# One order of waits and one DMA queue model in the planner of a two-branch attention kernel

## The chip, the cores and the metric

The kernel runs on one core of one Trainium2 chip. The time is that of the device for one execution, in microseconds (us); for the kernel before it is 681.26 us, the median of five runs (679.8 to 682.55). A difference of 0.2% (1.36 us) is about what can be told from no change.

Engines, by their short names: PE is TensorE (PEld its weight loads), ACT is ScalarE, DVE is VectorE, POOL is GpSimd, and SP is SyncE, whose only work here is to issue DMAs.

## The reference, cut to what matters

```python
x = A_x                                              # [1, 2048, 512], bf16, 32 heads of 16
g = sigmoid((x * gate_w).sum(-1, keepdims=True))
# branch A: softmax attention
q, k, v = split(x @ A_wqkv)                          # each [32 heads, 2048, 16]
o = softmax(q @ k.T * 16 ** -0.5) @ v
a = merge(o) @ A_wo
# branch B: linear attention
q, k, v = split(x @ B_wqkv)
pq, pk = phi(q), phi(k)                              # phi(t) = where(t > 0, t + 1, exp(t)) + 1e-6
num = pq @ (pk.T @ v);  den = pq @ pk.sum(rows) + 1e-6
b = merge(num / den) @ B_wo
return g * a + (1 - g) * b
```

## The kernel before, in words

Branch A makes 32 x 2048 x 2048 exponentials, and they are most of the work. They are cut into units of 128 keys x 512 queries of one head. Four heads make a round (there are 32 rounds of 64 units each, so 2048 units); a unit's scores are one matmul that reads `KT` and `Qz`. The exponential of a unit is made in one of two ways. ACT takes two units at a time from PSUM banks 0 and 1 or 2 and 3, as one `ACTIVATE` of 128x1024 that writes a slot of `P` (`cand_exp`, line 771 of the profile; "exp" below). Or DVE takes one unit from bank 4 or 5 by an addition that makes the bits of a power of two (`cand_op1`, line 685), and two shifted copies of it are made, by POOL (line 739) or by DVE (line 749), in tiles `Z`. PE then multiplies `P` and `Z` with the values `Vc` (`cand_pv`) and adds up in bank 7. A group of two matmuls for ACT and, mostly, one for DVE is called a score wave here (`cand_s`).

Everything else (projections, branch B, the final products) is written as tasks: generators that yield one step after another, with a round at which each is released and one at which it is due. Their steps fill the gaps. They share PSUM bank 6 until the very end (`owner`).

**The planner.** The function does not write instructions as it goes. It runs a model of the engines: each engine has a time at which it is free, each tile (`_Res`) the time at which its last writer and its readers end (`tw`, `tr`), and `_avail` gives the earliest start of a step on an engine. In a loop it collects what could be done next on each engine, picks one by the modelled start and by priorities, and emits it. So the order of instructions on every engine is fixed when the program is built, and it depends on the modelled durations. On the chip each engine goes through its own list in that order, held only by semaphores.

**Waits.** `deps_of` lists an instruction's dependencies: the writers of what it reads, then the writers and the readers of what it overwrites. `_Eng.add` (line 62) goes through that list, leaves out what the engine has already waited for, and keeps one wait for each semaphore, the highest value, in the order in which the semaphores first came up. A dependency is either an `_Ev` (an instruction of an engine) or a `_Raw` (a DMA's semaphore). `emit_engine` (line 1464) calls `wait_ge` for each wait and then the instruction. In the built program the first of the waits is carried by the instruction itself; the others, if there are any, go into one separate EVENT_SEMAPHORE instruction ahead of it, which belongs to line 1468. There are 716 of these on ACT, 578 on PE, 248 on POOL, 147 on DVE and 18 on SP.

**DMAs.** The planner's `dma` gives SP 60 ns for an issue (`issue`) and lets the data land a fixed time after it (`lat`), however many other DMAs were issued just before. Those that the loop at line 1450 issues on SP:

- `t_q` (names Q...): the projection of queries is written to `QT` by DVE (line 957) and spread to `Qz` by eight DMAs of 16 KB, `lat` 2500 ns; there are 15 such sets.
- `t_bout` (names BO...): for each of 16 row blocks, DVE writes the normalised branch-B rows to one of two slots `OBn`, which lie in the tile `wA0` (line 1163; the profile calls the tile `wA`), and a transposing DMA moves them to `OBT`, which lies in `xnat` (line 348), `lat` 3200 ns. The DVE step of block n overwrites the slot that the DMA of block n-2 reads, and so waits for it.
- `t_load` and `t_wo`: weights (WA, WB, WO) and rows of x (XN), `lat` 3500 and 5000 ns.
- `t_final` (names F...): the output rows, `lat` 2200 ns. `t_final` multiplies `OBT` and `OAT` with the output weights (line 377 through `mmt`) in bank 6.

The key lines of the waits and of the DMA model are

```python
        for d in deps:                                   # _Eng.add
            if d is None:
                continue
            ...
            start = max(E.free, _avail(E, reads, writes))    # dma
            E.free = start + issue
            fin = start + lat
```

Of the kernel before, what the change touches and what calls it, by code (L numbers as in the profile page):

```python
# [20 lines left out]
class _Raw:  # L21
    __slots__ = ("sem", "val")

    def __init__(self, sem, val):
        self.sem = sem
        self.val = val


class _Ev:
    __slots__ = ("E", "idx")  # L30

    def __init__(self, E, idx):
        self.E = E
        self.idx = idx


class _Eng:
# [23 lines left out]

    def add(self, fn, deps=(), inc=True, dma_sem=None):
        waits = []
        for d in deps:
            if d is None:
                continue
            if isinstance(d, _Raw):
                sem, val = d.sem, d.val
            else:
                sem, val = d.E.sem, d.E.cover(d.idx)  # L70
            key = id(sem)
            if val <= 0 or self.waited.get(key, 0) >= val:
                continue
            self.waited[key] = val
            for k, (s2, v2) in enumerate(waits):
                if s2 is sem:
                    if val > v2:
                        waits[k] = (sem, val)
                    break
            else:  # L80
                waits.append((sem, val))
        self.n += 1
        idx = self.n
        if inc:
            self.semval += 1
            self.inc_idx.append(idx)
            self.inc_val.append(self.semval)
        self.ops.append((waits, fn, inc, dma_sem))
        return _Ev(self, idx)


class _Res:

    __slots__ = ("name", "w", "r", "tw", "tr", "we", "late")
# [14 lines left out]
def _avail(E, reads, writes):  # L109
    t = 0.0  # L110
    for res in reads:
        if res.w is not None:
            x = res.tw if res.we is E else res.tw + LAT + (res.late if E.name == "pe" else 0.0)
            if res.we is E and E.name == "pe":
                x = 0.0
            if x > t:
                t = x
    for res in writes:
        if res.w is not None and res.we is not E:
            if res.tw + LAT > t:  # L120
                t = res.tw + LAT
        for e2, tr in res.tr.items():
            if e2 is not E and tr + LAT > t:
                t = tr + LAT
    return t


def bass_gated_mix__mha_block__linear_attn_block__prompt_kernel(
# [61 lines left out]
    with ExitStack() as es:  # L190
# [63 lines left out]
        SP = _Eng("sp", None, 0.0)  # L254
# [40 lines left out]
        def deps_of(E, reads, writes):  # L295
            deps = []
            for res in reads:
                if res.w is not None:
                    deps.append(res.w)
            for res in writes:  # L300
                if res.w is not None:
                    deps.append(res.w)
                deps.extend(res.r.values())
            if E is PE:
                deps = [d for d in deps if not (isinstance(d, _Ev) and d.E is PE)]
            return deps

        def emit(E, dur, fns, reads=(), writes=(), name=""):
            if callable(fns):
                fns = [fns]  # L310
            start = max(E.free, _avail(E, reads, writes))
            E.free = start + dur
            fin = start + dur + E.pipe
            deps = deps_of(E, reads, writes)
            if E is PO and gate[0] is not None:
                deps.append(gate[0])
            last[E] = None
            first = None
            for k, fn in enumerate(fns):
                ev = E.add(fn, deps if k == 0 else (), inc=(k == len(fns) - 1))  # L320
                if first is None:
                    first = ev
            last[E] = ev
            for res in reads:
                res.r[E] = ev
                res.tr[E] = fin
            for res in writes:
                res.w = ev
                res.we = E
                res.tw = fin  # L330
                res.r = {}
                res.tr = {}
            LOG.append((start, E.name, dur, name))
            RLOG.append((E.name, dur, E.pipe, [(d.E.name, d.idx) if isinstance(d, _Ev) else ("dma", id(d.sem), d.val) for d in deps if d is not None],
                         ev.idx, name, cur_mode[0] if E is PE else None))
            return fin

        dma_eng = {}

        def dma(E, o, i, sem, total, lat, reads=(), writes=(), transpose=False, noncontig=False, name="dma", issue=60.0):  # L340
            start = max(E.free, _avail(E, reads, writes))
            E.free = start + issue
            fin = start + lat
            eng = {"sp": nc.sync, "act": nc.scalar, "pool": nc.gpsimd}[E.name]

            def go():
                if transpose:
                    return eng.dma_start_transpose(o, i)
                if noncontig:
                    with nc.allow_non_contiguous_dma(reason="strided load"):  # L350
                        return eng.dma_start(o, i)
                return eng.dma_start(o, i)
            dd = deps_of(E, reads, writes)
            E.add(go, dd, inc=False, dma_sem=sem)
            raw = _Raw(sem, total)
            for res in reads:
                res.r[(E, id(sem))] = raw
                res.tr[(E, id(sem))] = fin
            for res in writes:
                res.w = raw  # L360
                res.we = SP if E is SP else None
                res.tw = fin
                res.r = {}
                res.tr = {}
            LOG.append((start, E.name, issue, name))
            RLOG.append((E.name, issue, lat, [(d.E.name, d.idx) if isinstance(d, _Ev) else ("dma", id(d.sem), d.val) for d in dd if d is not None],
                         ("dma", id(sem)), name, None))
            return fin
# [29 lines left out]
        for E, tbs in ((SP, (0, 1)), (AC, (2, 3))):  # L398
            for tb in tbs:
                dma(E, xnat[:, tb, :], x2[128 * tb:128 * (tb + 1), :], semX0[tb], 16, 3300.0, writes=[r_xn[tb]], issue=450.0)  # L400
        for k3 in (0, 1):
            dma(AC, wA0[:, :, k3, :], wsrc[:, :, k3 * D:k3 * D + 128], semW0[k3], 16, 3300.0, writes=[r_wA0[k3]], issue=450.0)
        for t in range(1, NQC):
# [5 lines left out]
            for h in range(2):  # L409
# [8 lines left out]
             reads=[r_ident], writes=[r_ident])  # L418
# [5 lines left out]
             reads=[r_pidx], writes=[r_pidx])  # L424
        emit(DV, 150, lambda: nc.vector.tensor_scalar(qmask[:, 1:2], pidx[:, 1:2], QS / 16.0, None, op0=ALU.mult),
             reads=[r_pidx], writes=[r_qmask])
        emit(DV, 150, lambda: nc.vector.tensor_scalar(qmask[:, 0:1], pidx[:, 1:2], -QS / 16.0, QS, op0=ALU.mult, op1=ALU.add),
             reads=[r_pidx], writes=[r_qmask])
# [5 lines left out]
        for (tile_, w_, rr) in ((bmask, 16, r_bmask), (zmask, 1, r_zmask)):  # L434
# [4 lines left out]
                reads=[rr], writes=[rr])  # L439
            emit(PO, 300, lambda ap=ap, w_=w_: nc.gpsimd.affine_select(  # L440
                out=ap, in_=ap, compare_op=ALU.is_ge, fill=0.0, base=15, pattern=[[16, 8], [0, w_]], channel_multiplier=-1),
                reads=[rr], writes=[rr])
        emit(PE, 3000, [mm(bank(b % 3 if b < 7 else 7), warm[:, 0:128], warm[:]) for b in range(8)], reads=[r_warm],
             writes=[r_bank[0], r_bank[1], r_bank[2], r_bank[7]])
# [140 lines left out]
        class C:  # L585
            __slots__ = ("E", "prio", "dur", "fns", "reads", "writes", "after", "name", "mode", "wt", "lock", "task")

            def __init__(self, E, prio, dur, fns, reads, writes, after, name, mode=None, wt=1.0, lock=False, task=False):
                self.task = task
                self.wt = wt  # L590
                self.lock = lock or E is PO
                self.E, self.prio, self.dur, self.fns = E, prio, dur, fns
                self.reads, self.writes, self.after, self.name, self.mode = reads, writes, after, name, mode
# [801 lines left out]
        while True:  # L1395
# [11 lines left out]
            for f in (cand_s, cand_dsolo, cand_pv, cand_op1, cand_shift, cand_pshift, cand_exp):  # L1407
                c = f()
# [8 lines left out]
            for c in cands:  # L1417
                a = _avail(c.E, c.reads, c.writes)
                start0 = start = max(c.E.free, a)
                if c.E is PE and c.mode and c.mode != st["mode"]:  # L1420
                    start = max(start, PE.free + SWITCH)
                if c.lock:
                    start = max(start, port["pool" if c.E is DV else "dve"])
# [7 lines left out]
                key = (max(start0, c.E.free + KEYW), -c.prio - (STICK if c.E is PE and c.mode == st["mode"] else 0.0))  # L1431
                if c.E not in by or key < by[c.E][0]:
                    by[c.E] = (key, start, c)
            key, start, c = min(by.values(), key=lambda v: v[1] - (BIAS if v[2].E is DV and v[2].lock else 0.0))
            if c.E is PE:
                fill(start, c.mode)
                start = max(start, PE.free + (SWITCH if c.mode and c.mode != st["mode"] else 0.0))
# [12 lines left out]
                port[c.E.name] = start + c.dur + 20.0  # L1450
            if isinstance(c.fns, tuple) and c.fns[0] == "DMA":
                _, o, i, sem, tot, lat, rd, wr, tr, chk = c.fns[1]
                fin = dma(SP, o, i, sem, tot, lat, reads=rd, writes=c.writes, transpose=tr, name=c.name)
                if not chk:
                    for res in wr:
                        res.tw = max(res.tw, fin)
            else:
                cur_mode[0] = c.mode
                fin = emit(c.E, c.dur, c.fns, c.reads, c.writes, name=c.name)
# [65 lines left out]
```

The softmax here doesn't subtract the row's maximum and nothing guards it: scores larger than these inputs give would overflow.

## Time and profile before

| | before |
|---|---|
| median of five runs | 681.26 us (679.8 to 682.55) |
| the profiled execution | 679.8 us |
| its span, first to last instruction | 677.7 us |
| granted PE clock | 1.00 |
| DMA, mean | 24 GB/s, 16 MB in all |

The profile counts an engine as busy from the start of an instruction to its end; on ACT and DVE the end of one overlaps the start of the next, so the mean duration of an exp, 1118 ns, is more than the 904 ns that lie between the starts of two exps that follow each other without a wait. A wait that an instruction carries itself is not shown as an instruction; an EVENT_SEMAPHORE is, as "PEldq L1468" or "DVEq L1468". The times of the planner and of the trace differ by a slowly growing offset (11.0 us at the trace's 551 us).

### The profile page before, as it was taken

To read this page: it belongs to the slowest core of one execution; us is meant where nothing else is said; L and a number is where in the kernel's file an instruction comes from. 1 tells how busy PE (TensorE), PEld (TensorE's weight loads), DVE (VectorE), ACT (ScalarE), POOL (GpSimd) and SP (SyncE) were. 2 spreads that over 40 slices of the span, in tenths; PEclk is the share of its full clock that TensorE was granted. 3 is DMA by queue.
4 is the path that set the end of the run, shared out by engine and by line. 5 is a ranking of instruction groups with operands and counts; after the bars stand their busy time and mean duration, and the time that the engine had idled before them with its cause. 6 is when DMAs were issued, how large, how long until landed. Compare 5 with 4: busy or idle time off the path is not lost.

```text
span 677.7 us, 24102 instructions
## 1 busy us (share of the span) xinstructions
PE 667.5 (98%) x9886; PEld 203.2 (30%) x9886; DVE 607.9 (90%) x1062; ACT 658.2 (97%) x734; POOL 550.7 (81%) x611
## 2 busy tenths in 40 slices
PE   8999999999999999999999999999999999999998
PEld 4322233323223232222333322232332332222222
DVE  6999999998899998999899888899998988899996
ACT  5899999999999999999999999999999999999995
POOL 3767878889878888888898888898788997887882
PEclk9999999999999999999999999999999999999999
DMA  6420001200000000000002000001020021000000
GB/s 133 134 89 8 4 2 38 66 10 3 2 10 1 10 2 2 10 2 2 12 3 65 10 10 1 10 17 22 7 34 9 14 48 31 17 16 11 26 17 32
DMA packets 27963, 15.96 MB, mean 24 GB/s; under 512 B 19792, under 2 KB 26832, under 8 KB 27856
## 3 DMA queue, kind: packets, MB, share of 16 engines
q1 hardware_dynamic: 26512, 13.91, 7.9%
q8 instruction: 79, 1.29, 0.8%
q10 hardware_dynamic: 1344, 0.52, 0.4%
q14 instruction: 28, 0.23, 0.1%
HBM read 6.69 MB, written 2.10 MB: 13 GB/s over the span
## 4 chain that ended last, share of the span: by engine, by line
PE 77%; ACT 13%; issue 5%; DVE 4%; DMA 0%; POOL 0%; ACTq 0%; DVEq 0%; POOLq 0%
PE ps L371 59%; PE ps L377 18%; ACT P L771 11%; DVE Z L685 2%; ACT eb L1056 1%; DMA xnat<-wA 0%; DVE T L1021 0%; DVE gnat L1013 0%; DVE QT L957 0%; DVE wA L1163 0%; PE ps L899 0%; DVE Z L749 0%; DVE OAT L1048 0%; POOL Z L739 0%; DVE rec L1040 0%
## 5 line engine op out<-in xcount | busy, mean ns | idle before, releaser
L771 ACT ACTIVATE P<-ps 128x1024 bf16<-128x1024 f32 x695 | 645.7, 1118 | 5.9 <-PE ps L371 5.8
L739 POOL TENSOR_TENSOR Z<-Z,mcon 128x512 int32<-128x512 int32 x465 | 480.4, 1058 | 81.4 <-DVE Z L685 49.1
L685 DVE TENSOR_SCALAR Z<-ps 128x512 int16<-128x512 f32 x659 | 441.0, 684 | 53.3 <-PE ps L371 45.3
L371 PE MATMUL ps<-Z,Vc 128*17 128x512 bf16 x1977 | 282.4, 382 | 0.3
L371 PE MATMUL ps<-Qz,KT 32*128 32x512 bf16 x2048 | 272.2, 384 | 3.4 <-DVE Z L685 1.0
L371 PE MATMUL ps<-P,Vc 128*17 128x512 bf16 x1389 | 250.1, 383 | 0.2
L371 PEld LDWEIGHTS ps<-Qz,KT 32*128 32x128 bf16 x2048 | 68.5, 91 | 259.2 <-ACT P L771 235.0
L371 PEld LDWEIGHTS ps<-Z,Vc 128*17 128x17 bf16 x1977 | 63.8, 88 | 79.4 <-issue 52.6
L749 DVE TENSOR_SCALAR Z<-Z 128x1024 int16<-128x1024 int16 x195 | 81.2, 432 | 0.2
L371 PEld LDWEIGHTS ps<-P,Vc 128*17 128x17 bf16 x1389 | 56.3, 88 | 55.4 <-issue 40.7
L371 PE MATMUL ps<-warm 128*32 128x512 bf16 (+15 forms) x600 | 62.4, 326 | 1.2 <-DVE dummy L420 1.2
L377 PE MATMUL ps<-xT,wA 128*32 128x512 bf16 (+1 forms) x528 | 43.9, 376 | 0.1
L1057 POOL TENSOR_SCALAR eb<-eb 128x512 f32<-128x512 f32 x32 | 20.2, 630 | 15.6 <-ACT eb L1056 9.1
L988 POOL TENSOR_SCALAR Vc<-Vc 128x576 bf16<-128x576 bf16 x32 | 21.7, 678 | 6.9 <-DVE Vc L985 3.4
L371 PEld LDWEIGHTS ps<-warm 128*32 128x32 bf16 (+1 forms) x600 | 20.3, 95 | 18.8 <-issue 12.3
L1021 DVE STREAM_TRANSPOSE T<-ps 128x512 f32<-128x512 f32 x32 | 22.6, 707 | 2.5 <-PE ps L377 2.3
L377 PE MATMUL ps<-wA,xnat 128*32 128x512 bf16 x256 | 22.6, 382 | 1.7 <-DVE wA L1163 1.7
L1044 POOL TENSOR_TENSOR T<-T,rg 128x256 bf16<-128x256 f32 x31 | 19.6, 631 | 5.7 <-DVE Z L749 2.6
L377 PE MATMUL ps<-phiK,xnat 128*32 128x512 bf16 x256 | 23.2, 383 | 0.0
L1056 ACT ACTIVATE eb<-ps 128x512 f32<-128x512 f32 x32 | 22.5, 703 | 0.0
L377 PE MATMUL ps<-wA,OAT 128*32 128x512 bf16 x256 | 22.5, 382 | 0.0
L377 PE MATMUL ps<-wB,xT 128*32 128x512 bf16 x256 | 22.4, 381 | 0.0
(79 smaller groups left out, 279.1 us busy)
## 6 DMA issues: line engine op xcount, KB each, us to landing
Qz<-QT SPq DMA_DIRECT2D x120, 16.0 KB, 1.8
wA<-in_A_wqkv_dram SPq DMA_DIRECT2D x4, 384.0 KB, 4.4
wB<-in_B_wqkv_dram SPq DMA_DIRECT2D x4, 384.0 KB, 3.3
xnat<-in_A_x_dram SPq DMA_DIRECT2D x3, 512.0 KB, 3.6
out_dram<-outt SPq DMA_DIRECT2D x12, 128.0 KB, 1.7
wA<-in_A_wo_dram SPq DMA_DIRECT2D x1, 512.0 KB, 3.7
wA<-in_B_wo_dram SPq DMA_DIRECT2D x1, 512.0 KB, 4.9
out_dram<-wA SPq DMA_DIRECT2D x4, 128.0 KB, 1.8
```

What stands on the lines that cost most here:

```text
L371: return lambda: nc.tensor.matmul(o, lhsT=l, rhs=r, start=start, stop=stop, skip_group_check=sg)
L377: h = nc.tensor.matmul(o[32 * j:32 * j + 32], lhsT=l[:, 32 * j:32 * j + 32], rhs=r, start=start, stop=stop, skip_group_check=True)
L685: return C(DV, OPP, 533 * n + 74, lambda: nc.vector.tensor_scalar(o, i, ZB, 0.0, op0=ALU.add, op1=ALU.max), [r_bank[b] for b in bks], r_Z[ ...
L739: return C(PO, 400, 70 + 484 * n, lambda: nc.gpsimd.tensor_tensor(Z[:, z, 0:512 * n].bitcast(I32), Z[:, z0, 0:512 * n].bitcast(I32), mcon[ ...
L749: return C(DV, 450 if hot else 300, 69 + 134 * n, lambda: nc.vector.tensor_scalar(Z[:, z, 0:512 * n], Z[:, z0, 0:512 * n], float(m), None, ...
L771: return C(AC, 500, 427 * n + 49, lambda: nc.scalar.activation(P[:, slot, 0:512 * n], bank(b0, n), ACT.Exp, scale=ESC), [r_bank[b0 + k] fo ...
L988: yield po(690, lambda k=k: nc.gpsimd.tensor_scalar(Vc[:, k, vs].rearrange("p a b c -> p (a b c)"), Vc[:, 0, vs].rearrange("p a b c -> p ( ...
L1021: yield dv(607, lambda: nc.vector.transpose(T1[:, a, :], bank(7)), [r_bank[7]], [r_T1[a]])
L1044: yield E(340 if r == NR - 1 else 640, lambda k=k: (nc.vector if r == NR - 1 else nc.gpsimd).tensor_tensor(dst_[:, k], src[:, k, :, 0:16], ...
L1056: yield ac(480, lambda: nc.scalar.activation(eb[:, i, :], bank(b), ACT.Exp), [r_bank[b]], [r_eb[i]])
L1057: yield po(640, lambda: nc.gpsimd.tensor_scalar(eb[:, i, :], eb[:, i, :], 1.0 + 1e-6, 0.0, op0=ALU.min, op1=ALU.max), [r_eb[i]], [r_eb[i]])
```

## The change

Every event gets the planned end of its instruction (`fin`), and `add` goes through the dependencies by falling planned end, with those on DMAs (`_Raw`) behind all others. The set of waits of an instruction stays the same; which of them comes first may differ. `dma` gets an occupancy `occ`: on SP, a DMA that has one lands `lat` after the time at which the queue is free, and keeps the queue for `occ`. The loop passes 1100 ns for transposes and for names that begin with W or X, and 650 ns for the rest; the DMAs issued ahead of the loop have none. The issue time in the model (60 ns) stays.

```diff
 class _Ev:
-    __slots__ = ("E", "idx")
-
-    def __init__(self, E, idx):
+    __slots__ = ("E", "idx", "fin")
+
+    def __init__(self, E, idx, fin=0.0):
         self.E = E
         self.idx = idx
+        self.fin = fin
...
     def add(self, fn, deps=(), inc=True, dma_sem=None):
         waits = []
-        for d in deps:
-            if d is None:
-                continue
+        for d in sorted([d for d in deps if d is not None], key=lambda d: -d.fin if isinstance(d, _Ev) else 0.0):
             if isinstance(d, _Raw):
                 sem, val = d.sem, d.val
...
                 ev = E.add(fn, deps if k == 0 else (), inc=(k == len(fns) - 1))
+                ev.fin = fin
...
+        q_free = [0.0]
+
-        def dma(E, o, i, sem, total, lat, reads=(), ..., name="dma", issue=60.0):
+        def dma(E, o, i, sem, total, lat, reads=(), ..., name="dma", issue=60.0, occ=0.0):
             start = max(E.free, _avail(E, reads, writes))
             E.free = start + issue
             fin = start + lat
+            if E is SP and occ:
+                q_free[0] = max(q_free[0], start) + occ
+                fin = q_free[0] - occ + lat
...
-                fin = dma(SP, o, i, sem, tot, lat, reads=rd, writes=c.writes, transpose=tr, name=c.name)
+                fin = dma(SP, o, i, sem, tot, lat, reads=rd, writes=c.writes, transpose=tr, name=c.name, occ=1100.0 if tr or c.name[0] in 'WX' else 650.0)
```

More of the change, by code (lines that the diff above doesn't have):

```diff
@@ L336, in emit, with dma @@
             return fin
-        dma_eng = {}
-        def dma(E, o, i, sem, total, lat, reads=(), writes=(), transpose=False, noncontig=False, name="dma", issue=60.0):
+        q_free = [0.0]
+        def dma(E, o, i, sem, total, lat, reads=(), writes=(), transpose=False, noncontig=False, name="dma", issue=60.0, occ=0.0):
             start = max(E.free, _avail(E, reads, writes))
```

## The prediction, made before the changed kernel was run

> **What bounds the kernel now.** I read the page first: the busy times, then the costliest groups.
>
> ```profile
> span 677.7 us, 24102 instructions
> PE 667.5 (98%) x9886; PEld 203.2 (30%) x9886; DVE 607.9 (90%) x1062; ACT 658.2 (97%) x734; POOL 550.7 (81%) x611
> ...
> L771 ACT ACTIVATE P<-ps 128x1024 bf16<-128x1024 f32 x695 | 645.7, 1118 | 5.9 <-PE ps L371 5.8
> ...
> L685 DVE TENSOR_SCALAR Z<-ps 128x512 int16<-128x512 f32 x659 | 441.0, 684 | 53.3 <-PE ps L371 45.3
> ```
>
> The reader is to see that the 695 exps alone fill 646 of 678 us and that ACT idled only 5.9 us before them. In the trace's start times 904 ns lie between two exps that do not wait, and 695 x 0.904 = 628 us; with 32 other ACTIVATEs of 0.48 us (15), the start (10) and the end after the last exp (9) that is 662 of 678. So the time is the exps plus what holds ACT up. Then the busy time of line 771 by stretches, and the chain of waits in the one that stands out (start, length, what):
>
> ```profile
> 200.00:300.00 100.00, 99.48 (x109) 1.00 0.02 5
> ...
> 556.00:562.00 6.00, 4.37 (x6) 1.00 0.32 67
> ```
>
> ```profile
> 556.35 3.18 DMA xnat<-wA
> 559.52 0.03 issue
> 559.55 0.02 DVEq L1468
> 559.57 0.04 issue
> 559.62 0.70 DVE wA L1163
> 560.32 0.14 issue
> 560.46 0.62 PE ps L377 x8
> ```
>
> At 556 us a transposing DMA of branch B holds DVE, DVE holds PE, PE holds ACT. The timelines of SP, DVE and ACT say for how long (in brackets the idle time before, and what ended it):
>
> ```profile
> 550.83 5.47 SPq L352 DMA_DIRECT2D Qz<-QT  x8
> 556.35 5.18 SPq L348 DMA_TRANSPOSE xnat<-wA  x3
> ```
>
> ```profile
> 559.62 0.69 DVE L1163 TENSOR_TENSOR wA<-ps,wA 128x512 bf16<-128x512 f32 x1 [2.04 <-DMA xnat<-wA]
> ```
>
> ```profile
> 561.49 2.98 ACT L771 ACTIVATE P<-ps 128x1024 bf16<-128x1024 f32 x3 [1.64 <-PE ps L371]
> ```
>
> The transpose of block 13 stood behind eight Qz loads on SP, and block 15's DVE step, which overwrites its slot, was placed as if it had not: 2.04 us lost on DVE, 1.64 us on ACT.
>
> **The queue model.** The rows of the DMAs themselves (duration of the issue, min/median/max ns):
>
> ```profile
> L352 SPq DMA_DIRECT2D Qz<-QT x120: 507/589/1445, 35.7 to 555.7; - x120
> ...
> L348 SPq DMA_TRANSPOSE xnat<-wA x16: 1188/1194/2050, 454.1 to 560.3; - x16
> ```
>
> A Qz issue takes 589 ns and a transpose 1194; the planner had 60, and the change's 650 and 1100 are close. Counted from the first Qz issue, before's plan issues the transpose 2.62 us later and lands it 3.20 after that, at 5.82. On the chip it landed 3.18 after 556.35, at 8.70. The new model gives 8 x 0.65 + 3.20 = 8.40. So block 15's DVE step moves 2.6 us later in the plan, other DVE work goes ahead of it, and its real wait falls from 2.04 to about 0.3 us, of which ACT should feel little: 1.64 - 0.15 = 1.5 us gained. Bounds: 1.64 gained if nothing is left, 0 if the stall moves whole to the next one in line. What is late next is the first output product (the eight matmuls at 560.46) and with it bank 6; it is planned against the same end, and nothing reads its rows before the end.
>
> No DMA is itself moved past another: SP's 153 direct and 28 transposing issues stay, with 60 ns in the plan. I went through the other users of a changed landing. A Qz half lands at most 7.05 us after its set is begun (7 x 650 + 2500) and the earliest planned reader comes 17.9 us after; most come 45 to 97 us after. WB loads among Qz sets land at most 2.5 us later, over 20 us before their reader. XN and WO have far more. The other transposes lie over 1.1 us apart with no Qz set ahead of them, and the output DMAs have no reader that follows soon. So the order should stay what it was up to about 556 us of the trace, and be made anew for the last 120 us. That remaking is the unknown. Its unit is an exp: if the plan gives DVE two units less, ACT makes one exp more, 0.904 us. Stretches of 56 us without other ACT work have 61, 61 and 61 exps, so the shares hardly wander; I take 0, with two exps either way (1.8 us) as bounds.
>
> Here the Trainium skill speaks against the change: "DMA: Bandwidth & Descriptors", section "Issuing engines are not separate DMA queues", holds that the sequencer's time to initiate a DMA is usually small beside the DMA itself. The row shows 589 ns against 1.8 us to landing, and eight of them in a line. By the page the loads would be out at once and this part would be worth 0, for a time of 680.8; by the row it is worth 1.5.
>
> **The order of waits.** From the built program's waits and the trace's semaphore times I took, for each first matmul of a PE step, the wait that came last. Where the engine was otherwise ready, its weights begin to load 41 ns after the last increment if the matmul carries that wait, and 104 ns after if the EVENT_SEMAPHORE does. In score waves of three matmuls the end comes 461 ns after the increment in one case (81 waves) and 548 in the other (24): a late wait in the wrong place costs 87 ns. Two such waves, wrong and right, in the weight loads' timeline:
>
> ```profile
> 592.21 0.13 PEld L371 LDWEIGHTS ps<-Qz,KT 32*128 32x128 bf16 x3 [0.45 <-ACT P L771]
> ...
> 593.10 0.10 PEld L371 LDWEIGHTS ps<-Qz,KT 32*128 32x128 bf16 x3 [0.42 <-ACT P L771]
> ```
>
> The upper starts 0.03 later and its loads take 0.03 longer. On PE the last wait is in the wrong place in 95 of 578. By the plan's own ends, sorting mends 90 of them, and spoils 29 of the others, where ACT or POOL really ended after the DVE that the plan expects last; most of those 29 have 100 ns or more to spare before PE itself is free. On POOL 68 starts come 66 ns earlier (134 to 68 ns), under 127 us of POOL idle time: nothing. If POOL were the bound that would be 4.5 us. On ACT the late wait is misplaced once; on DVE nine times, two of them mended and two others spoilt.
>
> For PE I count only what ACT feels. Behind mended waves stand 48 exps. 28 of them start over 10 ns after the wave's end because ACT is still busy: that cover is worth 28 x 87 = 2.4 us if it went. 20 start at once; 13 of these have a wave that really hung on the wait, and their ACT gaps, cut at 87 ns each, add up to 0.6 us. The spoilt waves have 24 exps behind them, and where the wait was the reason their slack leaves 0.07 us. I take -0.5 us. Bounds: -1.5 (1.0 if all 20 gain up to 87 ns, and half as much again through the mended steps ahead of a wave) and +0.9 (every spoilt wave pays what its slack does not cover).
>
> **Sum**, against the profiled execution: 679.80 - 1.5 - 0.5 + 0 = 677.8. That execution was the fastest of the five; the median lies 1.46 above, so 679.3 for a median, 0.29% less. Ends: -1.6 - 1.5 - 1.8 would be 676.4, and 0 + 0.9 + 1.8 would be 684.0; not all at once.
>
> **Rivals.** First, the stall moves and is not removed: block 15's step comes later, bank 6 is held until then, and the output products that follow push PE instead; only the waits' 0.5 is left: 681.26 - 0.5 = 680.8, no change that can be told. For it: bank 6 serves all tasks. Against it: after 100 us the waits show ACT idle at this one place and at the very end, although tasks have queued for bank 6 all along. Second, the planner's ends are poor and the spoilt waves pay in full: 681.26 - 1.5 + 0.9 = 680.7, no change. Against it: 90 mended to 29 spoilt. Third, slower: the last 120 us are made anew, and ACT gets more of the exps. 122 exps lie there now. From four more on (3.3 / 0.904 = 3.7) the gain is gone and 682.6 is passed; with five it is 679.3 + 4.5 = 683.8. For it: the planner picks by the next start, and nothing in it seeks few exps. Against it: the 61, 61, 61 above.
>
> **How the numbers follow.** Forecast 0.56, stall moves 0.20, poor ends 0.10, more exps 0.14. Differences within 0.2% (1.36 us: 679.9 to 682.6) can't be told from none. What the forecast loses to that band on its upper side it gets back from the middle cases' lower sides, so faster is 0.56; the middle cases are the same, 0.30; more exps is slower, 0.14. The predicted time is 679.3. The forecast's own range is 677.2 to 681.0; to hold 8 in 10 it reaches over the middle cases, 677.2 to 682.2.
>
> **What would show it.** Right: the DVE wait on the transpose at line 1163 goes from 2.0 to 0.3 us or less, and ACT's 1.64 is gone with nothing in its place; 695 exps within two; the same instructions up to some 556 us; fewer PE first loads 104 ns behind their last increment, below 45 of 578. Wrong: a new ACT gap of over 1 us after 556 us (first rival), or an order that differs well before 556 us, or exps up by four (third).

## The result, and the profile after

| | before | after |
|---|---|---|
| median | 681.05 us (59 runs, 679.31 to 684.14) | 678.86 us (34 runs, 677.24 to 681.44) |
| ratio of the times | | 0.9968, 95% interval 0.9961 to 0.9975 |
| the profiled execution | 679.8 us, span 677.7 us | 680.84 us, span 679.0 us |

By the ratio the changed kernel is 2.2 us faster (1.7 to 2.7). The profiled execution of it, 2 us above the median, was the third longest of the 34 and longer than the one shown of before. So its span can't be set against that of before; its stages can. First the page, busy times and the costliest groups:

```profile
span 679.0 us, 24111 instructions
PE 668.2 (98%) x9887; PEld 202.2 (30%) x9887; DVE 607.6 (89%) x1062; ACT 659.0 (97%) x735; POOL 552.1 (81%) x607
...
L774 ACT ACTIVATE P<-ps 128x1024 bf16<-128x1024 f32 x696 | 646.9, 1127 | 7.3 <-PE ps L374 7.2
L742 POOL TENSOR_TENSOR Z<-Z,mcon 128x512 int32<-128x512 int32 x461 | 480.3, 1067 | 78.0 <-DVE Z L688 59.9
L688 DVE TENSOR_SCALAR Z<-ps 128x512 int16<-128x512 f32 x657 | 439.4, 684 | 54.3 <-PE ps L374 46.5
```

Lines have moved by three. The exps went from 695 to 696, DVE's additions from 659 to 657. The two units that DVE makes less are one full exp more for ACT; the only exp of 128x512 is the last one in both kernels (at 668.7 us before, at 670.0 after). ACT's idle time before exps has grown from 5.9 to 7.3 us. Where ACT idled is told by the busy time of the exps in stretches (start and end, length, busy and count, clock, DMA share, GB/s):

```profile
200.00:300.00 100.00, 99.48 (x109) 1.00 0.02 5
556.00:562.00 6.00, 6.00 (x8) 1.00 0.30 55
```

A quiet stretch is as before to the digit; the one that stood out (4.37 us of 6 busy) is now full. The timelines of SP, DVE and ACT at that place:

```profile
553.09 5.70 SPq L355 DMA_DIRECT2D Qz<-QT  x8
558.83 5.34 SPq L351 DMA_TRANSPOSE xnat<-wA  x3
```

```profile
558.60 1.25 DVE L688 TENSOR_SCALAR Z<-ps 128x512 int16<-128x512 f32 x2
560.15 1.29 DVE L688 TENSOR_SCALAR Z<-ps 128x512 int16<-128x512 f32 x2 [0.30 <-PE ps L374]
561.66 0.69 DVE L688 TENSOR_SCALAR Z<-ps 128x512 int16<-128x512 f32 x1 [0.23 <-PE ps L374]
562.27 0.68 DVE L1166 TENSOR_TENSOR wA<-ps,wA 128x512 bf16<-128x512 f32 x1
```

```profile
555.54 12.97 ACT L774 ACTIVATE P<-ps 128x1024 bf16<-128x1024 f32 x14
```

The eight Qz loads still stand ahead of the transpose and still take 5.7 us. But block 15's step (line 1166, at 562.27) now comes after three more additions, and no idle time stands beside it. ACT runs 14 exps without a gap. Against that, the start went badly in this execution. The chain of waits from 18.88 us on, and ACT's timeline:

```profile
18.88 4.08 DMA gwc<-in_gate_w_dram
22.95 0.05 issue
23.01 0.61 POOL T L997
23.62 0.09 issue
23.71 0.73 POOL Vc L991
```

```profile
25.82 1.02 ACT L774 ACTIVATE P<-ps 128x1024 bf16<-128x1024 f32 x1 [3.48 <-PE ps L374]
27.95 2.00 ACT L774 ACTIVATE P<-ps 128x1024 bf16<-128x1024 f32 x2 [1.11 <-PE ps L374]
```

A load of the gate weights landed late, POOL waited for it and PE for POOL. Before's profiled execution lost 1.42 and 0.58 us at these two places.

From the start times of the exps every profiled execution can be cut into four stages, of which the first takes up these differences. The 21st exp lies just behind the first waits, the 561st ahead of the stall, the 591st behind it. All profiles of this study, in us:

| | ratio to before in time (95%) | start to 21st exp | 21st to 561st | 561st to 591st | 591st to end | 21st to end |
|---|---|---|---|---|---|---|
| before | 1 | 30.9 | 513.27 | 29.31 | 104.26 | 646.83 |
| after | 0.9968 (0.9961 to 0.9975) | 32.9 | 513.50 | 27.39 | 105.28 | 646.17 |
| e4_after_again | 0.9957 (0.9940 to 0.9973) | 31.4 | 513.28 | 27.39 | 105.28 | 645.95 |
| c0_base | 1.0023 (1.0011 to 1.0036) | 34.7 | 513.23 | 29.20 | 104.28 | 646.71 |
| c1_waits | 1.0030 (1.0015 to 1.0044) | 34.3 | 512.94 | 29.08 | 104.27 | 646.29 |
| c2_queue | 1.0005 (0.9991 to 1.0018) | 34.5 | 513.23 | 27.44 | 105.28 | 645.94 |
| c3_both | 1.0006 (0.9991 to 1.0021) | 34.8 | 512.95 | 27.67 | 105.27 | 645.89 |
| g_base | 0.9999 (0.9985 to 1.0013) | 31.2 | 513.24 | 31.06 | 104.28 | 648.58 |
| g_waits | 1.0002 (0.9986 to 1.0019) | 32.1 | 512.95 | 31.13 | 104.27 | 648.35 |
| g_queue | 0.9985 (0.9969 to 1.0000) | 30.9 | 513.24 | 27.38 | 105.29 | 645.91 |
| g_both | 0.9984 (0.9967 to 1.0001) | 33.7 | 512.88 | 27.81 | 105.26 | 645.95 |
| g_first | 0.9960 (0.9944 to 0.9975) | 31.8 | 513.25 | 27.45 | 104.27 | 644.96 |
| g_rpe | 1.0007 (0.9993 to 1.0021) | 31.6 | 514.07 | 30.73 | 104.31 | 649.11 |
| g_ract | 1.0019 (1.0007 to 1.0032) | 32.3 | 514.84 | 29.14 | 104.40 | 648.38 |

Where the edits of two kernels are alike, these columns mostly agree to 0.1 us, so they resolve what the times can't. The exception is the stage of the stall: with before's order it takes 29.1 to 29.3 us in four profiles and 30.7 to 31.1 in three.

The granted PE clock tells these apart. Up to 665 us the record of each profile has it at 1.0 or at 0.5, and it changes in steps of 3.41 us. In g_base, g_waits and g_rpe it is 0.5 for one such step right behind the stall (in g_base from 561.3 to 564.7 us); in before, c0_base, c1_waits and g_ract it stays at 1.0 there. The six profiles whose first stage took 32.9 us or more have a step at half clock in the start (after: from 25.4 to 28.8 us), and the eight others have none there. On the pages it stands as one digit below 9 in the row of forty slices, here of g_base and of after:

```profile
PEclk9999999999999999999999999999999998999999
```

```profile
PEclk9899999999999999999999999999999999999999
```

In all nine cases PE was idle for 1.50 to 2.57 us of the step of 3.41 us before. In the other steps up to 665 us it was idle for 1.42 us at most, but for one of 1.54 us in e4_after_again that no half clock followed. So it matters how the idle time of the stall falls on the steps: in g_base its 1.71 us lie within one, and in before its 1.67 us are split, 0.88 and 0.79. The same stall then costs about 1.8 us more. That the half clock is what makes it longer is inferred from these profiles; no run set it on purpose.

Each execution's mean clock is on record too, and one step at half clock makes 0.997 of it (0.5 x 3.41 / 680). The 59 runs of before above have no clock on record, but 104 others have, taken beside the later kernels: 35 are at 0.999 or 1.0, with a median of 680.1 us, 61 at 0.997, with 681.7, and 8 below. Of the changed kernel's 41 executions (e4_after_again included) 37 are at 0.999 or 1.0, with a median of 678.7 us, 4 at 0.997, with 681.1, and none below. In all kernels with the stall 12 of 176 executions are below 0.997, and in those without it none of 95.

### The profile page after: what moved, and what is told of

Its sections match the earlier page's. It is cut to its first block, busy times and chain, and to the rows that moved or that the text cites. A ratio compares the mean times of both kernels' runs of the same rounds, so it can differ in the third digit from the quotient of the medians.

```text
span 679.0 us, 24111 instructions
## 1 busy us (share of the span) xinstructions
PE 668.2 (98%) x9887; PEld 202.2 (30%) x9887; DVE 607.6 (89%) x1062; ACT 659.0 (97%) x735; POOL 552.1 (81%) x607
## 4 chain that ended last, share of the span: by engine, by line
PE 66%; ACT 19%; issue 6%; SPq 3%; DVE 2%; DMA 1%; POOL 1%; ACTq 0%; DVEq 0%
PE ps L374 51%; ACT P L774 18%; PE ps L380 15%; SPq L351 2%; ACT eb L1059 1%; DVE Z L688 1%; POOL Z L742 1%; DMA xnat<-wA 1%; DMA gwc<-in_gate_w_dram 1%; DVE wA L1166 0%; DVE gnat L1016 0%; DVE Z L752 0%; POOL Vc L991 0%; SPq L355 0%; DVE T L1024 0%
## 5 line engine op out<-in xcount | busy, mean ns | idle before, releaser
L752 DVE TENSOR_SCALAR Z<-Z 128x1024 int16<-128x1024 int16 (+1 forms) x197 | 82.8, 436 | 0.3
L380 PE MATMUL ps<-xT,wB 128*32 128x512 bf16 x256 | 22.3, 382 | 0.6 <-DVE wA L1166 0.6
```

The source lines that it names most:

```text
L380: h = nc.tensor.matmul(o[32 * j:32 * j + 32], lhsT=l[:, 32 * j:32 * j + 32], rhs=r, start=start, stop=stop, skip_group_check=True)
L752: return C(DV, 450 if hot else 300, 69 + 134 * n, lambda: nc.vector.tensor_scalar(Z[:, z, 0:512 * n], Z[:, z0, 0:512 * n], float(m), None, ...
```

## The experiments

**The changed kernel once more**, without an edit, to tell whether its late start belongs to it.

> The changed kernel once more, for a second profile. Theory: 2.0 to 2.4 us below before; the 3.5 us that ACT waits near 22 us in the first profile of the changed kernel belongs to a late load of gate_w in that execution, and is 1.0 to 2.0 us here as in the profile before. Rival (the change makes the start slower): again over 3 us.

Measured: 678.5 against 681.55 us. ACT waited again near 21 us, 3.31 us in one place, so the rival's figure for that gap came true. But the first stage took 31.4 us, against 32.9 in the first profile and 30.9 before: of the 2 us that the first profile lost there, 1.5 were gone. The gain of 3.0 us is above the expected 2.0 to 2.4; all six executions were at full clock, and only three of the eleven of before beside them (680.45 us). The start varies from one execution to the next, and is no price of the change that can be told from these two.

**The parts apart.** Four kernels: c0_base is the kernel before with plain copies in place of every transposing DMA, c1_waits has the sort alone, c2_queue the queue model alone, c3_both the two. The kernels further down keep these copies too, so none of them measures a part with the transposing DMAs in place.

```diff
                 if transpose:
-                    return eng.dma_start_transpose(o, i)
+                    w = 512 // parts                     # 3 for x, 2 for branch B
+                    for k in range(parts - 1):
+                        eng.dma_start(o[:, w * k:w * (k + 1)], i[:, w * k:w * (k + 1)]).then_inc(sem, 16)
+                    return eng.dma_start(o[:, w * (parts - 1):512], i[:, w * (parts - 1):512])
```

> The kernel before with each transposing DMA replaced by plain copies of the same bytes on the same queue (three for a load of x, two for a block of branch B), planned as before; the tokens of x after the first 512 and branch B's rows stay untransposed, so the values differ. It is the base for the next runs, which all have this. Expected by every theory: the order of all instructions as before, the DVE wait at line 1163 behind the eight Qz loads still there at 1.0 to 2.5 us, and a time within 1% of before.

> The base with the order of the waits alone (no queue model, so the same order of instructions). Theory (both parts help, the stall more): 0.2 to 0.9 us below the base, about 30 misplaced last waits on PE in place of 95, the DVE wait on branch B's copy as in the base. Rival A (the wait order does it all, the stall only moves): 1.8 to 2.4 below. Rival B (the queue model does it all): within 0.2 of the base.

> The base with the queue model alone (the changed kernel's order of instructions, before's order of waits). Theory: below the base by the base's ACT gap near 556 us less 0.1 to 0.6 us (half an exp more in the new plan), 1.0 to 1.8 us where that gap is 1.6, and no DVE wait on branch B's copy over 0.3 us. Rival A: within 0.3 of the base. Rival B: 1.8 to 2.4 below.

> The base with both parts, which is the changed kernel but for the copies. Theory: the two gains add up to within 0.5 us, 1.6 to 2.4 us below the base. Rival (the parts do the same work twice): no more than the larger of the two. ACT's wait near 22 us for the load of gate_w: if the change causes it, it is over 3 us here and under 2 in the base; if it is the execution's, the two do not differ by rule.

Does c0_base stand for the kernel before? Its DVE and ACT timelines at the stall:

```profile
563.29 0.69 DVE L1167 TENSOR_TENSOR wA<-ps,wA 128x512 bf16<-128x512 f32 x1 [1.93 <-DMA xnat<-wA]
```

```profile
565.16 5.73 ACT L775 ACTIVATE P<-ps 128x1024 bf16<-128x1024 f32 x6 [1.52 <-PE ps L375]
```

It does there: 1.93 and 1.52 us for 2.04 and 1.64. Its start is 3.8 us longer (with a step at half clock), and its time 0.23% above before. Now c2_queue, ACT's timeline over the same place:

```profile
555.09 15.70 ACT L780 ACTIVATE P<-ps 128x1024 bf16<-128x1024 f32 x17
```

The 17 exps follow each other without a gap: the queue model alone removes the stall. In the table the third stage falls by 1.76 us and the last grows by 1.00; in time, 1.0005 against 1.0023 is 1.2 us less, though the intervals overlap. The half exp more that the expectation counts is a whole one, as in the changed kernel. The sort alone leaves the stall where it was (29.08), takes 0.29 us from the 540 exps between the 21st and the 561st, and in time nothing is to be seen (1.0030 against 1.0023). With both, the second stage keeps the sort's gain (512.95), but the third gives it back (27.67 against 27.44), and from the 21st exp to the end the sort is worth nothing on top of the queue model: 645.89 against 645.94, and in time 1.0006 against 1.0005. The chain of waits in c3_both, ahead of the place of the stall, shows who takes it back:

```profile
546.89 0.47 SPq L354
547.36 0.04 issue
547.40 3.94 DMA xnat<-wA
551.34 0.03 issue
551.37 0.05 DVEq L1475
551.42 0.04 issue
551.46 0.70 DVE wA L1170
```

DVE's step for another block waits for an earlier copy of branch B, 0.4 us in this kernel and 0.2 in c2_queue. That copy lands 3.9 us after its issue, where the median is 1.9, so DVE, a little earlier thanks to the sort, only comes to it earlier. PE waits for this step:

```profile
552.21 0.83 PE L384 MATMUL ps<-xT,wA 128*32 128x512 bf16 x12 [0.27 <-DVE wA L1170]
```

In g_both, further down, the same wait of PE is 0.40 us; c2_queue and g_queue have none there. The third stage is 0.23 and 0.43 us longer in the two kernels that have it. The mending itself came: first matmuls of a PE step whose last wait sits in the EVENT_SEMAPHORE: 94 in c0_base, 34 in c1_waits, 98 in c2_queue, 30 in c3_both.

**The same four with an earlier load of the gate weights.** The start of the c kernels was held by the load that had held the changed kernel's. It is issued on SP ahead of the last twelve copies of x:

```diff
+        SP.ops.insert(11, SP.ops.pop(15))                # the load of gwc
         def emit_engine(E, eng):
```

> The base with the load of gate_w issued on SP ahead of the last twelve copies of x instead of behind them; nothing else moves. Theory (POOL waits for this load, PE for POOL and ACT for PE, in every kernel so far, and that is what made the starts differ): POOL's 2.8 us wait and most of ACT's 4.1 us wait near 22 us are gone, 2.5 to 4.0 us below the base. Rival (the start is held by the copies of x themselves): within 0.7 us of the base.

> The base with gate_w early, and the order of the waits alone. With the start out of the way the times should resolve what the traces show. Theory: 0.3 to 0.6 us below the base with gate_w early (the trace of the same kernel with gate_w late gave 0.4 us after the first 30 us). Rival A (the queue model does it all): within 0.15 us of it. Rival C (the wait order is worth what I took from misplaced waits times 87 ns, 90 x 0.087 less 29 x 0.087): 5 us below it.

> The base with gate_w early, and the queue model alone. Theory: 1.2 to 1.7 us below the base with gate_w early (ACT's gap of 1.6 us near 562 us gone, half an exp of 0.45 more at the end, part of it hidden behind the last exps). Rival (the new plan of the last 120 us gives the gain back): within 0.4 us.

> The base with gate_w early and both parts. Theory: the sum of the two within 0.4 us, 1.6 to 2.2 us below the base with gate_w early, and 4 to 6 below the base. Rival: no more than the larger of the two.

POOL's wait for that load went, but ACT still waited 3.08 us near 22 us. The chain of waits of g_base tells for what:

```profile
19.49 1.37 SPq L351
20.86 0.04 issue
20.90 0.43 SPq L351
21.34 0.04 issue
21.38 1.79 DMA xT<-in_A_x_dram
23.17 0.04 issue
23.22 1.05 PE ps L381 x16
```

The next to hold the start is SP itself, which issues the x copies until 21.3 us. In time g_base lies 0.24% under c0_base, 1.6 us, measured on another chip, each against before: less than the expected 2.5 to 4.0 us and more than the rival's 0.7. The rival was right in that the copies of x are next in line.

The parts repeat. Sort: 0.29 us less in the second stage (g_waits) and 0.36 (g_both); in time nothing (1.0002 against 0.9999), and on top of the queue model nothing either (645.95 against 645.91 us from the 21st exp on, 0.9984 against 0.9985 in time). Queue model: time 0.9985 against 0.9999, 1.0 us less; last stage 1.01 us more. But the stage of the stall falls by 3.68 us here, twice as much as in the c kernels, though only the place of one early load on SP differs. DVE lost no more than before (2.02 us); its step was followed by three gaps on ACT in place of one, the second in and the third just behind the step at half clock (561.3 to 564.7 us):

```profile
562.50 1.02 ACT L775 ACTIVATE P<-ps 128x1024 bf16<-128x1024 f32 x1 [2.09 <-PE ps L375]
564.02 1.02 ACT L775 ACTIVATE P<-ps 128x1024 bf16<-128x1024 f32 x1 [0.50 <-PE ps L375]
565.47 2.85 ACT L775 ACTIVATE P<-ps 128x1024 bf16<-128x1024 f32 x3 [0.42 <-PE ps L375]
```

**One copy moved, everything else as before.** If the eight Qz loads ahead of block 13's data are the whole matter, it is enough to let that data pass four of them on SP, in before's own order:

```diff
+        SP.ops.insert(k13 - 4, SP.ops.pop(k13))          # k13: block 13's, right behind the eight Qz loads
         def emit_engine(E, eng):
```

> g_base (copies in place of the transposing DMAs, gate weights earlier on SP) with the model, the sort and the order of the kernel before, except that on SP the first copies for block 13 are issued ahead of the last four Qz loads. Theory (the stall behind the eight Qz loads is the whole of what the queue model is worth): DVE's wait on a copy for block 15 falls from 2 us or more to under 0.3 us, ACT's loss between 556 and 566 us from 1.8 to 3.5 us to under 0.3, the exps stay at 695, and the ratio to before is 0.996 to 0.9985 (g_base 0.9999, g_queue 0.9985). Rival (the remade order of the last 120 us is what is worth something, and the stall only moves, to the Qz loads or to the output products): ratio 0.999 to 1.001, and a new ACT gap of over 1 us after 556 us.

SP's and ACT's timelines of g_first:

```profile
551.73 2.45 SPq L356 DMA_DIRECT2D Qz<-QT  x4
554.34 0.93 SPq L351 DMA_DIRECT2D xnat<-wA  x1
555.31 0.60 SPq L352 DMA_DIRECT2D xnat<-wA  x1
555.96 2.50 SPq L356 DMA_DIRECT2D Qz<-QT  x4
```

```profile
554.18 14.83 ACT L775 ACTIVATE P<-ps 128x1024 bf16<-128x1024 f32 x16
```

No gap in 16 exps, and no idle time before DVE's step for block 15; third stage 27.45, as with the queue model, last stage 104.27, as before. The time is 678.56 against 681.68 us, 0.9960, or 2.7 us under g_base by the ratios, measured on another chip. So the loads ahead of block 13's data are the cause, and the stall does not move when it is removed. The remade order of the last 120 us is no gain but a price: its last stage is 1.0 us longer. The times say the same, with more noise. All six executions of g_first were at full clock, and are 1.3 us under the four of before that were too (679.83 us); g_queue's nine at full clock are 0.2 us under before's twelve. As 0.3 us of the price come back outside of the span (see the sum below), the stages make that difference 0.7 us, and these few executions 1.1.

**The order of waits, turned round.** Two kernels built on g_waits, to price the misplaced wait by making it common:

```diff
-... key=lambda d: -d.fin if isinstance(d, _Ev) else 0.0):
+... key=lambda d: (d.fin if self.name == 'pe' else -d.fin) if isinstance(d, _Ev) else 0.0):    # g_rpe
+... key=lambda d: (d.fin if self.name == 'act' else -d.fin) if isinstance(d, _Ev) else 0.0):   # g_ract
```

> g_waits with the order of the waits turned round on PE alone (the wait planned to end last goes into the separate EVENT_SEMAPHORE), sorted on ACT, DVE and POOL. Theory (most of a late start on PE is hidden because ACT is still busy): of some 161 score waves that hang on a wait each starts and runs 60 to 90 ns later, 11.8 us in all if ACT felt every one; by the slack of the exps behind them ACT feels 0.1 to 1.0 us, so 0.1 to 1.0 us above g_waits (ratio to before 1.0003 to 1.0015). PE first loads with the late wait misplaced: some 480 of 574. Rival (every wave pays): 6 to 12 us above g_waits, ratio 1.009 to 1.018.

> g_waits with the order of the waits turned round on ACT alone (so that the late wait for PE's scores goes into the EVENT_SEMAPHORE), sorted on the others. Theory (ACT sets the time and the waits on it count where the exp is otherwise ready): some 249 exps have under 61 ns of slack and each loses up to 61 ns, 9 us in all (6 to 12) above g_waits, ratio to before 1.009 to 1.018. Rival (ACT's sequencer has handled the semaphores before ACT is free, so the place of the wait costs nothing): within 1 us of g_waits, ratio 0.9987 to 1.0017.

g_rpe: the late wait is now in the wrong place in 543 of 578 PE steps instead of 36, and the second stage is 1.12 us longer than in g_waits; in time 1.0007 against 1.0002. The theory's 0.1 to 1.0 us held in time and was a little low for the stage; the 6 to 12 us of the rival are excluded.

g_ract: here the theory fell. All 716 late waits on ACT are in the wrong place. Exps that hang on their wait start 82 ns after PE's increment instead of 22, as expected. But the second stage is 1.9 us longer and the time 0.0017 (1.2 us; 2.4 among the nine and the four executions at full clock, each set against before's), not 9. The rival (nothing, because the sequencer runs ahead) doesn't describe it either, as the 82 ns show. What happened is told by the times from PE's last increment to the start of the exp, over the exps from 30 to 545 us:

| | exps | that start within 10 ns of the lowest | median time from increment to start | lowest |
|---|---|---|---|---|
| g_waits | 542 | 98 | 120.5 ns | 22 ns |
| g_ract | 540 | 94 | 185.5 ns | 82 ns |

The number of exps that start on the wait is nearly the same, and the median has moved by 65 ns. My reading of this, which no run tests by itself: ACT runs its list some 60 ns later against PE most of the time, and not 60 ns later with each exp; an exp that starts late leaves the next one, whose scores came no later, that much less to wait. The 1.9 us are some 30 delays of 60 ns. My estimate had added up 60 ns for every exp without slack, as if PE moved along each time. The groups of exps on the pages of g_waits and g_ract agree with that:

```profile
L778 ACT ACTIVATE P<-ps 128x1024 bf16<-128x1024 f32 x695 | 646.5, 1134 | 8.7 <-PE ps L378 8.6
```

```profile
L778 ACT ACTIVATE P<-ps 128x1024 bf16<-128x1024 f32 x695 | 646.3, 1089 | 7.3 <-PE ps L378 6.5
```

The idle time before exps is 1.4 us shorter in g_ract, of which its shorter stage of the stall (29.14 against 31.13 us, without the step at half clock) explains 2.0; the rest is some 0.6 us more, and nothing near 9.

## Why the prediction was right, and where it was not

The time was forecast at 679.3 us and is 678.86; the likeliest case is the one that came. By its steps:

- **What bounds the kernel.** Right: ACT's exps 904 ns apart, and one stall that could go. 109 exps in the same 100 us before and after.
- **The queue model, the stall.** The mechanism is right, and g_first shows it by itself. The size was low: 1.5 us forecast, 1.92 measured from the 561st to the 591st exp. The step that was off is the 0.15 us left to ACT: nothing was left, and the short gaps after the stall, which the single row of 1.64 does not hold, went with it (all of ACT's loss between 556 and 566 us: 2.03 before, 0.09 after). The first rival, that the stall only moves, is out.
- **An order unchanged up to 556 us.** Right: the two kernels' first differences stand at 559.6 us on DVE, 560.4 on PE, 561.6 on POOL, and on ACT at 668.7.
- **The last 120 us made anew.** Taken as 0 with 1.8 either way; it cost 1.0 us. DVE makes two additions less and ACT one exp more, which is the unit that the prediction names, at 0.904 us. It went to the side of the third rival, with one exp in place of its four. Stall and remade order together were -1.5 in the prediction and are -0.9 in the profiles.
- **The order of waits.** This is the step that failed: -0.5 us forecast, nothing found. The mending itself came as said (on PE 95 misplaced waits went to 30 of 574, on POOL 108 to 8), and so did the cover: 0.3 us in the second stage, 1.1 us for 500 more misplaced waits. But the prediction took what ACT gains as gained for good. On top of the queue model it is lost again, in c3_both and g_both to within 0.05 us, at a late transfer where the chain was followed. In the changed kernel the second stage shows no gain at all (513.50 and 513.28 for 513.27). The chain of waits near 505 us in the first profile of it:

```profile
500.59 4.67 DMA xnat<-wA
505.27 0.03 issue
505.29 0.05 DVEq L1471
505.34 0.04 issue
505.39 0.70 DVE wA L1166
```

  DVE waits 0.82 us there for a transpose, and ACT 0.43 us at 507 us. In the profile of before DVE waited 0.22 us at the same step and ACT did not feel it; the prediction had passed over the place. In the second profile of after ACT lost 0.24 us near there, with PE last and not the transpose, so this is settled for the first alone. POOL's part was not tried by itself.
- **The sum.** From the 21st exp on, the two profiles of after are 0.7 and 0.9 us shorter than that of before. The times give 2.2 (1.7 to 2.7). Two things make up most of the difference, and the prediction has neither. The time of an execution less its span is 2.1 us in every kernel with before's order and 1.8 in every one with the new order, 0.3 us more gained; what passes there the profile doesn't tell. And the changed kernel has a step at half clock less often. At full clock it is 1.3 us faster (678.7 against 680.1 us); the other 0.9 is that 66% of before's executions with a clock on record had such a step and 10% of the changed kernel's, at some 1.6 us each (estimates from the medians above). Without the stall PE's idle time there is gone, and the start is the one place where the profiles of kernels without it still show such a step. Where the steps of before's executions lie is not shown, for the only one that was profiled has none; g_base, g_waits and g_rpe show one behind the stall.
- **Luck.** So the forecast of 2.0 us is nearer to the times than its terms deserve: the sort's 0.5 did not come, the new order cost 1.0, and what made up for them was not in the sum. The 1.46 us from the profiled execution to the median were carried over to the changed kernel as noise. By the clocks above they were probably the half clock, and the changed kernel's median lies 0.1 us above its median at full clock.

The Trainium skill, "DMA: Bandwidth & Descriptors", section "Issuing engines are not separate DMA queues", was weighed in the prediction and would have made the queue part worth nothing. The measurement decides against that here: moving one copy past four loads of 0.6 us each on SP took away the whole stall.

**A version better than both** follows from g_first: before's plan with block 13's transpose four places earlier on SP, and no more. From the stages one would expect it to be 0.7 us faster than the changed kernel, the 1.0 us of the last stage less the 0.3 outside of the span. It was not tried with transposing DMAs; copies stand in for them in g_first.

## What to carry to other kernels

Where a planner fixes the order, model each DMA queue as serial, and look for the one consumer that stands behind a burst; moving that one transfer ahead of half the burst was worth some 0.7 us more here than planning everything anew. Price a delay per instruction only after asking whether it is paid each time: in a loop whose producer does not wait for the late one, 61 ns on 540 exps cost 1.9 us and not 9. Cut the trace into stages by the work done (the n-th exp), because a start that varies by 2 us hides much of the rest in the spans. And compare executions of the same granted clock: the same stall took 1.7 to 2.0 us of ACT's time at full clock and 3.3 to 3.6 where a step at half clock came behind it.

## What the runs showed of the hardware

- A wait in a separate EVENT_SEMAPHORE mostly costs 60 ns or more over one that the instruction carries. The shortest times from the increment to the start: 22 ns carried (g_waits) against 82 (g_ract) on ACT, 42 against 105 on PE (g_rpe), 53 against 131 on POOL (before). Four of the 95 such starts on PE in before came 59 ns after it.
- Two DMAs of the same kind and size, with nothing queued close ahead of them on SP, can take very different times to land: the transposes between 498 and 508 us of the first profile of after took 2.4 (lowest and median) to 4.7 us. It is the same one each time: the second of these four took 4.1 us in before and 4.5 in e4_after_again, the others 2.4. Why was not tried.
- The first 21 exps took 30.9 to 32.9 us in three profiles of kernels that are alike there, by when the loads of x and of the gate weights land.
- PE's granted clock went to 0.5 for 3.41 us behind a step of 3.41 us in which PE idled for 1.50 us or more, nine times in the fourteen profiles up to 665 us. Behind one other step, with 1.54 us idle, it did not, nor behind idle time that was split over two steps (0.88 and 0.79 us in before).
